# Moving broadcasts, bias blocks and the last loads of an attention stage by a step on one DMA queue

## The chip, the cores and the metric

One kernel runs on one core of a Trainium2 chip. The metric is the device time of one execution in microseconds (us); of several executions the median is taken. The engines are TensorE (PE; its weight loads are PEld), VectorE (DVE), ScalarE (ACT), GpSimd (POOL) and SyncE (SP). SP computes nothing: its queue issues nearly all DMAs of this kernel, in program order, and an issue that must wait holds everything behind it.

## The reference

Two layers in sequence, all in float32.

- Attention with a learned position bias: 4 batches, 8 heads, 576 positions, 64 values a head. The scores are `q k^T / 8` plus a bias that depends on the head and on the two positions: `x = log1p(|i - j|) / log1p(max(i, 1))`, `h = relu(x w1 + b1)` with 32 hidden units, `bias = h w2`. Then a softmax over each row, with `exp(...) / (sum + 1e-9)`, and the product with v.
- A rational expert layer on the 2304 x 512 result x: `h = x w_in` (to 2048), `g = P(h) / (Q(h) + 1e-6)` with a cubic P and a `Q = 1 + |b0| |h| + |b1| h^2`, and `g w_out` (back to 512).

## The kernel before, in words

**Bias stage.** For 36 groups of 16 rows the kernel computes the bias of all heads (`relu` L594 on VectorE and ScalarE, matmuls L640, scaling L646 on ScalarE) and stores it to five tables in DRAM, `tab[0]` to `tab[4]` (L652). The groups are taken in the order 0 to 15, 32 to 35, 16 to 31 (L617), so `tab[4]`, which holds the last 64 rows, is done early. The tile `e` that a store reads has five buffers. `load_bias(p, c)` (L250) reads block c of head pair p from the tables back into an SBUF tile, skewed: three DMAs for c = 0 to 3, six for c = 4. The dictionary `done` (L618) says after which group's store a block of the first pair is read.

**Attention stage.** Heads are taken in pairs; a pair and a batch make a unit u, 16 in all, in the order of pairs. A unit has four blocks of 128 rows; the last 64 rows of two units share a step. So two units take nine steps, a group g, and `step_a(i)` (L498) writes out the work of all 72 steps, NS = 72, as a pipeline: scores of step i (`e_qk` L320, PE L333), bias and row minimum (`e_ttr` L338, DVE L343), exponential with row sums (`e_exp` L352, ACT L359), transposes of step i - 2 (`e_tp` L394) and the product with v of step i - 3 (`e_pv` L430). VectorE copies the products into `xs` (L452; three buffers). The order of the calls is the order on each engine's queue; nothing is reordered.

What each step issues on SP:

- `loads(i)` (L477): q and k of a coming unit (L264, L265; two buffers each), v, a block of the next pair's bias (at steps 2, 5, 8, 10 and 13 of each pair's 18), and at step NS - 7 `load_x(0, 0)` (L277, L283), which reads the first tokens of the attention result back for the expert layer.
- When a unit's last block is through, `e_recip` (L367) inverts its sums, PE transposes them, VectorE copies them to `rt` (L425), and SP writes them to DRAM, `rs` (L428, at the end of the step).
- `load_rb(u)` (L372) reads `rs` back, broadcast to 64 partitions: four DMAs (L378, L382). The first waits until the write of `rs` has landed. In program order it comes one step after that write.
- `e_norm(u)` (L387) multiplies `xs` by the broadcast, on POOL (for u = NX = 12 on VectorE), and SP stores the result, `xd` (L392). It comes five steps after the `load_rb`.
- `run_jobs` (L468) advances a background queue of weight conversion by one VectorE operation a step: loads `wx` and `wy` (L129, L130), operations on VectorE, ScalarE (`wh`, L146) and POOL (L167), and stores of the parts (L171, L107, L108, and L227 for reads of parts stored before).

In the steps i = NS - 5 to NS - 2, `split_x` (L287) splits the first tokens into two parts: a cast on ScalarE (L294, `xh`) ahead of the step's exponentials, and a subtraction on VectorE (L295, `xl`) a step later. At step NS - 1 come `load_x(1, 1)` and the first matmuls of the expert layer, `mm1(0, 0)` (L300, PE L309).

**Expert layer.** It follows from L683 on: 48 sections of h matmuls (L309), rational function on ScalarE, POOL and VectorE, and output matmuls (L770).

Of the kernel before, what the change touches and what calls it, by code (L numbers as in the profile page):

```python
# [33 lines left out]
def tile_attn_moe(  # L34
# [32 lines left out]
    def tab_rows(c, h):  # L67
        n, w, o = P if c < 4 else 64, H * TW - 1, h * TW + S - 1 - P * c
        flat = tab[c].rearrange("r h x -> (r h x)")
        return flat[o:o + n * w].rearrange("(r w) -> r w", w=w)[:, :S]  # L70
# [158 lines left out]
    with tc.manual_schedule():  # L229
# [3 lines left out]
        with ExitStack() as actx:  # L233
# [16 lines left out]
            def load_bias(p, c):  # L250
                if c == 0:
                    bias[p] = bpool.tile([P, 10, S], F32, tag="bias", name=f"bias{p}")
                t = bias[p]
                r0, r1 = tab_rows(c, 2 * p), tab_rows(c, 2 * p + 1)
                for o, x, y, r in ((5 + c, 0, S, r1[:, 0:S]), (c, 64, S, r0[:, 0:512]), (c, 0, 64, r0[:, 512:S])):
                    n = P if c < 4 else 64
                    for z in range(0, P, n):
                        nc.sync.dma_start(out=t[z:z + n, o, x:y], in_=r)

            def load_qk(u, eng=nc.sync):  # L260
                p, b = units[u]
                q = qkp.tile([P, S], F32, tag="q", name=f"q{u}")
                k = qkp.tile([P, S], F32, tag="k", name=f"k{u}")
                eng.dma_start(out=q, in_=qt[b, p])  # L264
                eng.dma_start(out=k, in_=kt[b, p])  # L265
                qk[u] = (q, k)

            def load_v(u, eng=nc.sync):
                p, b = units[u]
                t = vpool.tile([P, 5, P], F32, tag="v", name=f"v{u}")  # L270
                eng.dma_start(out=t, in_=vp[b, p].rearrange("(c k) d -> k c d", k=P))
                vt[u] = t
# [14 lines left out]
            def split_x(n_, k):  # L287
                if k == 0:
                    pool = xps[n_ % 2]
                    xh[n_] = pool.tile([P, KD, TT], F32R, tag="xh", name=f"xh{n_}")  # L290
                    xl[n_] = pool.tile([P, KD, TT], F32R, tag="xl", name=f"xl{n_}")
                hi, lo, x = (v[n_][:, k, :] for v in (xh, xl, xr))
                return (
                    lambda: A.copy(out=hi, in_=x),  # L294
                    lambda: V.tensor_tensor(out=lo, in0=x, in1=hi.bitcast(F32), op=ALU.subtract),  # L295
                )
# [159 lines left out]
            NS = len(steps)  # L456
            later = []
            NU = len(units)
# [18 lines left out]
            def loads(i):  # L477
                g, c = divmod(i, UPG)
                if i == 1:
                    load_qk(1, nc.scalar)  # L480
                    load_v(1, nc.scalar)
                u = 2 * g + 2
                if c == (5 if g else 7) and u < NU:
                    load_qk(u)
                if c == (6 if g else 7) and u < NU:
                    load_v(u)
                if g and c == 0:
                    load_qk(u - 1)
                if g and c == 2:
                    load_v(u - 1)  # L490
                p, r = divmod(i, 2 * UPG)
                r = {2: 0, 5: 1, 8: 2, 10: 3, 13: 4}.get(r)
                if r is not None and p + 1 < NP:
                    load_bias(p + 1, r)
                if i == NS - 7:
                    load_x(0, 0)

            def step_a(i):  # L498
                def ok(d):
                    return 0 <= i - d < NS  # L500

                if i < NS:
                    loads(i)
                first = []
                if NS - 5 <= i < NS - 1:
                    first = split_x(0, i - NS + 5)
                if first:
                    first[0]()
                    later.append(first[1])
                while len(later) > (1 if i < NS - 1 else 0):  # L510
                    later.pop(0)()
                if ok(0):
                    e_qk(i)
                if ok(1):
                    e_exp(i - 1, 1)
                run_act()
                if i >= TL:
                    mx = ps_mx.tile([P, 2, 512], F32, tag="mx", name=f"mx{i}")
                tails = pv = None
                if ok(TL):  # L520
                    tails = e_tp(i - TL, mx)
                if i == NS + 1:
                    mm1(0, 1)
                if ok(TL + 1):
                    pv = e_pv(i - TL - 1, mx)
                if ok(0):
                    for j in range(2):
                        e_ttr(i, j)
                    e_exp(i, 0)
                if ok(1):  # L530
                    u, c = steps[i - 1]
                    if c == (3 if u % 2 else 4):
                        e_recip(u)
                if i == NS - 1:
                    load_x(1, 1)
                    mm1(0, 0)
                g, c = divmod(i - TL, UPG)
                if g > 0:
                    u = 2 * g - 2
                    if c == 1 and u != NX or i == NS + TL:  # L540
                        e_norm(u)
                    if c == 5 and g * 2 < NU:
                        e_norm(u + 1)
                    if c == 0 and u + 1 < NU - 1:
                        load_rb(u + 1)
                if i == NS - 8:
                    e_norm(NX)
                if g < NU // 2 and c == (5 if g else 7):
                    load_rb(2 * g)
                if i >= 2:  # L550
                    run_jobs(i >= 5 and (c > 0 or g % 2 == 0))
                if tails:
                    tails()
                    if i == NS + TL - 1:
                        load_rb(NU - 1)
                if pv:
                    pv()

            with ExitStack() as bctx:
# [55 lines left out]
                bg = in_order(bg, after)  # L615

                order = [*range(16), *range(32, NG), *range(16, 32)]  # L617
                done = {10: 0, 18: 1, 22: 4, 30: 2}  # L618
                for n in order[:LEAD]:
                    relu(n)  # L620
                for y, n in enumerate(order):
                    if y == 4:
                        load_v(0)
                    if y + LEAD < NG:
                        relu(order[y + LEAD])
                    i0 = NROW * n
                    mid = i0 + NROW - 1
                    pool, nm = (ps_sc, "sc")
                    if y == NG - 1:
                        pool, nm = (ps_mx, "mx")  # L630
                    elif y % 3 == 1:
                        pool, nm = (ps_tp, "tp")
                    pa = pool.tile([P, 2, 512], F32, tag=nm, name=f"pb{n}")
                    cuts = sorted({0, mid, 512, EW})
                    for a, z in zip(cuts, cuts[1:]):
                        o = pa[:, a // 512, a % 512:a % 512 + z - a]
                        for c in range(4):
                            x = rows[n, c]
                            x = x[:, a - mid:z - mid] if a >= mid else x[:, mid - a:mid - z:-1]
                            T.matmul(  # L640
                                o[32 * c:32 * c + 32], w28[:, 32 * c:32 * c + 32], x,
                                start=True, stop=True,
                            )
                    e = rpool.tile([P, EW], F32, tag="e", name=f"e{n}")
                    z = 1 if ENG[n][3] == "A" else 0
                    A.activation(  # L646
                        out=e, in_=pa.rearrange("p a s -> p (a s)")[:, :EW], func=AF.Identity,
                        bias=c8[:, z:z + 1], scale=rts[:, n:n + 1],
                    )
                    g, k = divmod(n, 8)  # L650
                    x0 = S - NROW - i0
                    nc.sync.dma_start(  # L652
                        out=tab[g][NROW * k:NROW * k + NROW, :, x0:x0 + EW].rearrange("r h x -> (r h) x"),
                        in_=e,
                    )
                    if y in done:
                        load_bias(0, done[y])
                    if y == NG - 1:
                        load_bias(0, 3)
                    if y >= NG - EARLY:  # L660
                        step_a(y - NG + EARLY)
                A.activation(out=babs, in_=abs_[:, 4:6], func=AF.Abs)
# [274 lines left out]
```

## Time and profile before

| what | value |
|---|---|
| time, median of 3 executions | 731.99 us (731.96 to 733.12) |
| the profiled execution | 728.89 us, of which its span is 727.1 us |
| PE busy | 683.4 us (94% of the span), 6450 instructions |
| DVE busy | 576.1 us (79%) |
| ACT busy | 486.4 us (67%) |
| POOL busy | 232.4 us (32%) |
| mean granted clock of TensorE | 0.981 |
| DMA | 129.69 MB, mean 178 GB/s |

The span runs from the first to the last instruction; the execution's own time is 1.8 us longer. Busy shares are means over the whole span, which has three stages: the bias stage to about 58 us, the attention steps to about 313 us, then the expert layer. Issues of DMAs don't count as busy, so SP has no row here: its work is read from its timeline and from the waits of its queue.

### The profile page before, as it was taken

What the parts mean: (1) busy time and instruction counts of PE and PEld (TensorE: products, weight loads), DVE (VectorE), ACT (ScalarE), POOL (GpSimd) and SP (SyncE); (2) the same over time, 40 slices, a digit from 0 to 9 for tenths busy, and PEclk for the clock granted to TensorE, in tenths of its full rate; (3) what the DMA queues carried; (4) which work ended last, traced back from release to release, by engine and by line L of the source; (5) the groups of instructions that cost most, each with busy time, mean ns of one, the idle gap of its engine ahead of it and who ended that gap; (6) DMA issues with size and microseconds to landing.
All of it is one profiled execution on the core that took longest, in us unless ns stands there. A gap on an engine that the chain in (4) does not pass through costs nothing.

```text
span 727.1 us, 16614 instructions
## 1 busy us (share of the span) xinstructions
PE 683.4 (94%) x6450; PEld 582.7 (80%) x6450; DVE 576.1 (79%) x1032; ACT 486.4 (67%) x758; POOL 232.4 (32%) x144
## 2 busy tenths in 40 slices
PE   6989998979899698699999999999999999999997
PEld 4757876757677586589899998999999999989996
DVE  7976876847677386549999999999986978778766
ACT  6878886868678486567666576766575565656552
POOL 0000221212122120116444545454444444444442
PEclk9999999999999799999999999999999999999999
DMA  4888877877787888625445444369851303032021
GB/s 165 287 293 295 281 225 246 277 235 237 228 279 237 250 275 277 188 87 171 153 142 166 164 136 136 131 189 281 272 172 44 129 2 131 22 109 72 17 87 44
DMA packets 98159, 129.69 MB, mean 178 GB/s; under 512 B 12177, under 2 KB 60577, under 8 KB 98081
## 3 DMA queue, kind: packets, MB, share of 16 engines
q1 hardware_dynamic: 96704, 126.96, 53.5%
q10 hardware_dynamic: 1376, 1.67, 0.7%
q8 instruction: 51, 0.84, 0.5%
q14 instruction: 28, 0.22, 0.1%
HBM read 89.85 MB, written 35.61 MB: 173 GB/s over the span
## 4 chain that ended last, share of the span: by engine, by line
PE 70%; DMA 11%; DVE 4%; issue 2%; SPq 2%; ACT 1%; POOL 0%; DVEq 0%; ACTq 0%; POOLq 0%
PE o L770 26%; PE h L309 26%; PE mx L442 8%; PE sc L333 7%; DMA k<-in_kt_dram 4%; PE tp L402 3%; DMA wih<-wh 2%; DMA rs<-rt 1%; DMA bias<-tab 1%; DMA xd<-xs 1%; DMA ws<-wh 1%; PE mx L402 1%; DVE s L343 1%; DMA xr<-xd 1%; DVE gh L718 1%
## 5 line engine op out<-in xcount | busy, mean ns | idle before, releaser
L343 DVE CUSTOM_DVE_ANT_0 s<-sc,bias 128x576 f32<-128x576 f32 x144 | 103.3, 754 | 57.2 <-PE sc L333 42.3
L700 POOL TENSOR_TENSOR u<-u,w 128x768 f32<-128x768 f32 x48 | 97.2, 2025 | 155.9 <-ACT u L698 155.8
L333 PE MATMUL sc<-k,q 64*128 64x288 f32 (+1 forms) x640 | 96.0, 435 | 17.7 <-DMA k<-in_kt_dram 17.2
L359 ACT ACTIVATE p<-s,m 128x576 f32<-128x576 f32 x144 | 110.5, 771 | 1.3 <-DVE m L343 1.0
L697 ACT ACTIVATE w<-h 128x768 f32<-128x768 f32 x48 | 39.0, 813 | 101.5 <-PE h L309 101.5
L739 POOL TENSOR_TENSOR gl<-m,r 128x768 fp32r<-128x768 f32 x47 | 87.2, 1856 | 55.1 <-DVE m L732 48.7
L410 ACT COPY pt<-tp 128x1024 f32<-128x1024 f32 x72 | 72.6, 1008 | 43.1 <-PE tp L402 42.8
L442 PE MATMUL mx<-pt,v 128*64 128x128 f32 (+1 forms) x1600 | 99.7, 275 | 0.9 <-DVE xs L452 0.9
L309 PE MATMUL h<-xh,wih 128*128 128x384 f32 x288 | 97.3, 338 | 0.0
L309 PE MATMUL h<-xh,wil 128*128 128x384 f32 x288 | 97.0, 337 | 0.0
L309 PE MATMUL h<-xl,wih 128*128 128x384 f32 x288 | 96.9, 336 | 0.0
L442 PEld LDWEIGHTS mx<-pt,v 128*64 128x64 f32 x1600 | 82.7, 142 | 6.3 <-ACT u L698 1.1
L770 PE MATMUL o<-woh,gh 128*128 128x512 f32 x216 | 85.2, 395 | 0.0
L770 PE MATMUL o<-wol,gh 128*128 128x512 f32 x216 | 85.1, 394 | 0.0
L333 PEld LDWEIGHTS sc<-k,q 64*128 64x128 f32 (+1 forms) x640 | 51.9, 179 | 40.2 <-issue 11.8
L704 ACT ACTIVATE r<-u,qc 128x768 f32<-128x768 f32 x48 | 45.1, 940 | 37.3 <-POOL u L700 37.2
L708 DVE TENSOR_TENSOR t<-t,h 128x768 f32<-128x768 f32 x48 | 45.6, 949 | 29.3 <-ACT t L699 23.8
L725 DVE SCALAR_TENSOR_TENSOR m<-u,qc,gh 128x768 f32<-128x768 f32 x48 | 63.0, 1313 | 5.0
L732 DVE SCALAR_TENSOR_TENSOR m<-t,cst,m 128x768 f32<-128x768 f32 x48 | 65.2, 1358 | 1.7
L718 DVE SCALAR_TENSOR_TENSOR gh<-t,cst,r 128x768 fp32r<-128x768 f32 x48 | 53.2, 1109 | 8.2 <-ACT r L705 5.8
L770 PE MATMUL o<-woh,gl 128*128 128x512 f32 x216 | 56.2, 395 | 0.0
L309 PEld LDWEIGHTS h<-xh,wih 128*128 128x128 f32 x288 | 54.1, 188 | 1.8 <-issue 0.3
(71 smaller groups left out, 1286.7 us busy)
## 6 DMA issues: line engine op xcount, KB each, us to landing
tab<-e SPq DMA_DIRECT2D x36, 295.5 KB
wx<-in_w_in_dram SPq DMA_DIRECT2D x16, 512.0 KB
wy<-in_w_in_dram SPq DMA_DIRECT2D x16, 512.0 KB
wx<-in_w_out_dram SPq DMA_DIRECT2D x16, 512.0 KB
wy<-in_w_out_dram SPq DMA_DIRECT2D x16, 512.0 KB
xr<-xd SPq DMA_DIRECT2D x8, 768.0 KB
ws<-wh SPq DMA_DIRECT2D x20, 256.0 KB
ws<-wl SPq DMA_DIRECT2D x20, 256.0 KB
```

The source lines that it names most:

```text
L309: T.matmul(hps[s][:, j, :TT], w[:, k, sl], x[:, k, :], start=(k == 0 and z == 0), stop=(k == KD - 1 and z == 2),)
L333: T.matmul(sc[i, j][o, a, :SH], q[r, x], k[r, a * SH:(a + 1) * SH], start=True, stop=True,)
L343: V.tensor_tensor_reduce(out=t.rearrange("p (a s) -> p a s", a=2), in0=sc.pop((i, j))[:, :, :SH], in1=bias[p][:, 5 * j + c, :].rearrange(" ...
L359: A.activation(out=prob[i][:, z * S:z * S + S], in_=t, func=AF.Exp, bias=m, scale=-1.0, accum_out=sums[u % 4][:, k:k + 1],)
L410: A.copy(out=t[:, 0:8].rearrange("p x (r s) -> p r x s", r=2), in_=ps)
L442: T.matmul(ps[y, o], vt[n][:, kc, y], t[:, 2 * kc + j if kc < 4 else 8, o], start=(kc == 0), stop=(kc == 4),)
L700: G.tensor_tensor(out=u, in0=u, in1=w, op=ALU.mult)
L718: V.scalar_tensor_tensor(out=hi, in0=rt[s, "t"], scalar=abs_[:, 0:1], in1=rt[s, "r0"], op0=ALU.add, op1=ALU.mult,)
L725: V.scalar_tensor_tensor(out=m, in0=rt[s, "u"], scalar=qc, in1=rt[s, "gh"].bitcast(F32), op0=ALU.add, op1=ALU.mult,)
L732: V.scalar_tensor_tensor(out=m, in0=rt[s, "t"], scalar=abs_[:, 0:1], in1=m, op0=ALU.add, op1=ALU.subtract)
L739: eng.tensor_tensor(out=lo, in0=rt[s, "m"], in1=rt[s, "r0"], op=ALU.mult)
L770: T.matmul(po[n, c], l[:, j, c * P:(c + 1) * P], r[fp][:, j, :], start=(first and x is a), stop=(last and x is z),)
```

## The change

No instruction is added or taken away; only places in the order change.

- `load_rb` is called one step later, for odd units (c == 0 to c == 1) and for even ones (c == 5 to c == 6; 7 to 8 in the first group).
- The bias blocks of the next pair are loaded at steps 3, 7, 8, 12 and 16 of a pair's 18, not 2, 5, 8, 10 and 13.
- `load_x(0, 0)`, the four `split_x` of the first tokens and `e_norm(NX)` come one step later each.
- Block 4 of the first pair's bias is read behind block 3, after the last group, not after the 23rd (y = 22).

```diff
--- before.py
+++ after.py
@@ -489,10 +489,10 @@
                 if g and c == 2:
                     load_v(u - 1)
                 p, r = divmod(i, 2 * UPG)
-                r = {2: 0, 5: 1, 8: 2, 10: 3, 13: 4}.get(r)
+                r = {3: 0, 7: 1, 8: 2, 12: 3, 16: 4}.get(r)
                 if r is not None and p + 1 < NP:
                     load_bias(p + 1, r)
-                if i == NS - 7:
+                if i == NS - 6:
                     load_x(0, 0)
 
             def step_a(i):
@@ -502,8 +502,8 @@
                 if i < NS:
                     loads(i)
                 first = []
-                if NS - 5 <= i < NS - 1:
-                    first = split_x(0, i - NS + 5)
+                if NS - 4 <= i < NS:
+                    first = split_x(0, i - NS + 4)
                 if first:
                     first[0]()
                     later.append(first[1])
@@ -541,11 +541,11 @@
                         e_norm(u)
                     if c == 5 and g * 2 < NU:
                         e_norm(u + 1)
-                    if c == 0 and u + 1 < NU - 1:
+                    if c == 1 and u + 1 < NU - 1:
                         load_rb(u + 1)
-                if i == NS - 8:
+                if i == NS - 7:
                     e_norm(NX)
-                if g < NU // 2 and c == (5 if g else 7):
+                if g < NU // 2 and c == (6 if g else 8):
                     load_rb(2 * g)
                 if i >= 2:
                     run_jobs(i >= 5 and (c > 0 or g % 2 == 0))
@@ -615,7 +615,7 @@
                 bg = in_order(bg, after)
 
                 order = [*range(16), *range(32, NG), *range(16, 32)]
-                done = {10: 0, 18: 1, 22: 4, 30: 2}
+                done = {10: 0, 18: 1, 30: 2}
                 for n in order[:LEAD]:
                     relu(n)
                 for y, n in enumerate(order):
@@ -657,6 +657,7 @@
                         load_bias(0, done[y])
                     if y == NG - 1:
                         load_bias(0, 3)
+                        load_bias(0, 4)
                     if y >= NG - EARLY:
                         step_a(y - NG + EARLY)
                 A.activation(out=babs, in_=abs_[:, 4:6], func=AF.Abs)
```

## Rows read from the trace of the kernel before

**Rows 1.** Page, part 4: shares of the chain that ended last, by engine.

```profile
PE 70%; DMA 11%; DVE 4%; issue 2%; SPq 2%; ACT 1%; POOL 0%; DVEq 0%; ACTq 0%; POOLq 0%
```

**Rows 2.** Timeline of PE: start us, us, instructions, [idle before <-releaser].

```profile
64.25 1.24 PE L333 MATMUL sc<-k,q 64*128 64x288 f32 x8
...
108.22 1.24 PE L333 MATMUL sc<-k,q 64*128 64x288 f32 x8 [1.01 <-DMA k<-in_kt_dram]
...
124.04 1.19 PE L333 MATMUL sc<-k,q 64*64 64x288 f32 x14 [2.22 <-DMA k<-in_kt_dram]
...
276.70 1.24 PE L333 MATMUL sc<-k,q 64*128 64x288 f32 x8
...
313.44 0.44 PE L309 MATMUL h<-xh,wih 128*128 128x384 f32 x1
```

**Rows 3.** Waits, 108 to 277 us: who waited for whom: us, times, longest.

```profile
PE sc L333 <- DMA k<-in_kt_dram: 15.6, 7, 6.3
...
PEld sc L333 <- DMA q<-in_qt_dram: 8.2, 3, 4.5
...
PE mx L402 <- DVE xs L452: 4.3, 4, 2.6
...
ACT wh L146 <- DMA wih<-wh: 6.8, 4, 3.4
...
POOL xs L391 <- DMA rb<-rs: 17.6, 4, 6.9
```

**Rows 4.** Waits of SP's own queue, 108 to 277 us.

```profile
SPq L378 <- DMA rs<-rt: 40.4, 11, 4.9
```

**Rows 5.** Timeline of SP: one broadcast and what stands around it; one late broadcast.

```profile
106.92 2.82 SPq L428 DMA_DIRECT2D rs<-rt  x1
109.84 0.37 SPq L392 DMA_DIRECT2D xd<-xs  x1
...
114.14 0.45 SPq L378 DMA_DIRECT2D rb<-rs  x1
...
118.14 0.42 SPq L265 DMA_DIRECT2D k<-in_kt_dram  x1
...
277.56 0.60 SPq L382 DMA_DIRECT2D rb<-rs  x1
```

**Rows 6.** SP's issues by line: count, ns min/median/max, first and last start.

```profile
L258 SPq DMA_DIRECT2D bias<-tab x72: 319/584/1692, 23.0 to 234.9; - x72
...
L129 SPq DMA_DIRECT2D wx<-in_w_in_dram x16: 379/426/1000, 64.8 to 460.6; - x16
```

**Rows 7.** Windows 58:108, 58:313: busy by engine, PEclk, DMA share, GB/s.

```profile
58.00:108.00 50.00, 48.97 (x778) 39.14 (x778) 38.89 (x122) 44.27 (x90) 7.06 (x6) 1.00 0.82 266
58.00:313.00 255.00, 225.46 (x3448) 181.18 (x3450) 174.37 (x538) 190.63 (x377) 44.09 (x33) 0.95 0.78 250
```

**Rows 8.** Timelines of SP, ACT, PE, DVE: block 4 of the first pair, and after.

```profile
38.43 4.61 SPq L258 DMA_DIRECT2D bias<-tab  x6
...
62.02 2.69 SPq L258 DMA_DIRECT2D bias<-tab  x6
...
46.95 1.61 ACT L646 ACTIVATE e<-pb,c,cst 128x591 f32<-128x591 f32 x2 [3.18 <-DMA tab<-e]
...
47.85 5.93 PE L640 MATMUL pb<-ring,w 128*32 128x447 f32 x96 [2.83 <-ACT e L646]
...
49.84 1.27 DVE L602 TENSOR_SCALAR ring<-lts,nts 128x496 f32<-128x496 f32 x3 [1.30 <-PE pb L640]
...
70.37 0.44 DVE L141 TENSOR_SCALAR wk<-wx 128x512 uint32<-128x512 uint32 x1 [0.35 <-DMA wx<-in_w_in_dram]
```

**Rows 9.** Timelines of SP and ACT at the end of attention.

```profile
285.99 0.33 SPq L392 DMA_DIRECT2D xd<-xs  x1
...
292.72 0.57 SPq L283 DMA_DIRECT2D xr<-xd  x1
...
297.96 0.51 ACT L294 CAST xh<-xr 128x384 fp32r<-128x384 f32 x1 [7.54 <-DMA xr<-xd]
```

## The prediction

> **What bounds the kernel now.** I began with the chain of work that ended last: TensorE carries 70% of it and DMAs 11% [rows 1], so beside the matmuls it is transfers that set the end. The windows of the page show TensorE solid from about 360 us on, so the transfers must be on the chain in the attention stage. I read TensorE's timeline there and noted when each of the 72 attention steps starts its scores. From step 4 to step 18 it takes 43.97 us with one wait of 1.01, so 42.96/14 = 3.07 us a step: the pace TensorE can keep. Steps 18 to 64 take 168.48 us where 46 x 3.07 = 141.2 would do: 27.2 us lost. From step 64 to the first matmul of the expert layer it takes 36.74 us where 8 x 3.07 = 24.6 would do: 12.2 us lost [rows 2].
>
> The waits say who is late in that stretch: TensorE waits for k (15.6 us), for q (8.2) and for VectorE's xs copy (4.3); ScalarE waits for the store of an earlier wh before it may write that tile again (6.8 in four waits) [rows 3]. The late parties are SP's DMAs. SP's own waits name the reason: of 169 us it spends 40.4 in 11 waits at L378, for the write of the inverted sums to land before it may read them back as a broadcast [rows 4]. One such place: the rs write is issued until 109.74, one xd store follows, then nothing until the broadcast at 114.14; the k that step 22 needs stands behind it, goes out at 118.14, and TensorE stands still for it until 124.04 [rows 2, 5]. In program order that k belongs to step 18, which began at 108.22: SP runs 10 us behind the step it serves.
>
> **SP's budget** decides. From 108.2 to 277.6 I add up SP's DMA issues: 178 of them take 105 us (the first and the last of them: [rows 5]). With the 40.4 of broadcast waits that is 145.4 us for steps whose matmuls need 141.2. SP can't catch up, whatever it is late by stays, and each further wait of its own (the remaining 24 us) is passed on.
>
> **The change, part by part.**
>
> *Broadcasts a step later.* load_rb issues four DMAs on SP and nothing else. They move behind the jobs of the old step and behind the loads and the xd store of the next; no instruction is added. The rs write needs the same time to land, but SP now issues other DMAs meanwhile. A bias DMA takes 0.584 us at the median, a wx or wy 0.43 [rows 6], an xd 0.37 [rows 5]. For the 11 waits I count what now stands between rs and rb that did not before: six bias DMAs (3.5 us) for rs2, rs6, rs10 (block 4) and for rs4, rs8 (blocks 1 and 2); three bias DMAs and xd (2.1) for rs5, rs9; wx, wy and xd (1.2) for rs3 and rs7; about 1 us of stores or loads for rs11 and rs12, as there is no bias left to load by then. At 3.7 us a wait (40.4/11) that leaves 0.2 us for each of the first five, 1.6 for the next two, 2.5 and 2.7 for the last pairs: 14.6, and with the uneven waits some 16 of the 40.4 us. So 24 us of SP's time are free.
>
> SP then needs 105 + 16 = 121 us for 141 us of steps. It gains nearly 5 us in each group of nine steps, and q and k, issued four steps (12.3 us) before their scores, land in time: k5 took from 118.14 to 124.04, 6 us with its queueing [rows 2, 5]. The stores of wh and xd, late by the same lag, come early too. Bounds for this stretch: all 27.2 us at best; at worst a third of it, 9, if the transfers' own time keeps the rest (first rival). I take 21: SP enters the stretch 8 to 10 us late, so the first waits for k stay in part, and in the last pair, where nothing fills the waits, some come back. The 1.01 us wait ahead of step 18 [rows 2] I count as gone; bounds from 1 slower to 1 faster.
>
> The rs write is out at 109.74 and its reader at 114.14, 4.4 us [rows 5]. The Trainium skill, "DMA: Bandwidth & Descriptors", in its anatomy of one DMA (measured on GpSimd's path), puts the fixed cost at about 2 us, most of it the receipt of the write; the trace here has twice that, with whatever was queued ahead. At 2 us no wait would be left and the stretch would come to its best bound, 6 us under my sum.
>
> *Bias blocks moved* from 2, 5, 8, 10, 13 to 3, 7, 8, 12, 16 of each 18 steps. The same 18 DMAs, all SP's. Taking six of them from in front of the q and k of step 14 and putting them into a wait costs nothing. Block 4 is now loaded six steps (18.4 us) before its use, against a lag of 10, an issue of 3.5 and a landing of 4.4 like that of rs: just covered even if SP never catches up; uncovered, VectorE would wait the shortfall, three times.
>
> *First pair's last block behind the fourth.* Now its six DMAs hold SP from 38.43 for 4.61 us among the table stores; behind them ScalarE waits 3.18 us for a table store to free its buffer, TensorE 2.83 for ScalarE, VectorE 1.30 for TensorE [rows 8]. The gain lies between the 1.30 that reached VectorE and TensorE's 2.83: I take 2.0. At its new place the block's six DMAs (instead of three of the next pair's block 0) stand ahead of the first wx: three DMAs more at 0.45 (2.69/6), 1.35 us. VectorE already waits 0.35 for that wx at 70.37 [rows 8], so I give back 1.4. The block itself is due at step 6, about 71 us; it would be out by 66.1 (62.02 + 9 x 0.45) and landed by 70.5. Sum 0.6 faster; bounds 2.8 faster (no wx wait) and 1.5 slower.
>
> *The end of attention, a step later.* e_norm(12) is one VectorE multiply and an xd store, now issued behind rs13 and v15; load_x is one SP DMA; each of the four splits is a ScalarE cast and a VectorE subtraction. Now xd goes out at 285.99, the read of it at 292.72 and the first cast at 297.96, after ScalarE waited 7.54 us [rows 9]. All three move by one step together, so that chain of 12 us (6.7 for the write to land, 5.2 for the read) stays. With SP on time xd can go out some 4 us into step 65 (an estimate: one step and the multiply), the read lands 16 us into it, and the split of step 68 begins 9.2 us into it: ScalarE still waits 6 to 7 us. That gains 1. Of the 12.2 us lost here 4.7 are more than this wait; I put them down to the lag, as in the stretch before, and count 4. Together 5; bounds 8 faster (half the wait gone as well) and 1 slower (the last split, now in step 71, delays the first matmul). rb14 moves behind two reads of x: hidden, as its multiply comes three steps later; uncovered, it would cost the 2 us of four issues.
>
> Sum: 21 + 1 + 0.6 + 5 = 27.6 us less. The profiled execution took 728.89 us, so 701.3; it lies 3.1 below the median of the runs, 731.99. Taken from the median: **704.4 us**.
>
> **Rivals.**
>
> *The DMA engines bind* (0.20). From 58 to 313 us they are busy 0.78 of 255, 199 us of work; the 70 steps at full pace leave 215, a share of 0.93. In the one long stretch nearly without stalls the share is 0.82 [rows 7]. If that is all these packets allow, 199/0.82 = 243 us instead of 255: a gain of 12, 720 us. Against it: SP's empty waits hold the share down now. The Trainium skill's same page ("Issuing engines are not separate DMA queues") speaks for this rival: time saved on a sequencer is usually small beside the DMA itself; SP's 105 us of issuing in 169 speak against it.
>
> *Slower: the broadcast reaches POOL late* (0.05). POOL multiplies five steps after the broadcast's place, after the change four (12.3 us); it already waits 17.6 us for rb [rows 3]. If SP stays 10 us late, four issues (0.45 to 0.60 each [rows 5]) and a landing of 4.4 make 16.5, and xs is stored 3 us later than now; VectorE's copy then waits for its tile, and TensorE for the copy. If four of the units pass on 3 us each: 12 slower, 744 us. It decides from a lag of about 6 us on. Against it: rb waits for the rs write before and after, so even a late SP issues it hardly later than now.
>
> *No change* (0.09): the waits only move, to the wx loads and wh stores that SP would then reach too early, and q and k stand behind those as they stand behind rb now: 731 us. For it: the 24 us of other waits.
>
> The forecast has 0.66.
>
> **The numbers.** The best bounds together give 731.99 - 27.2 - 1 - 2.8 - 8 = 693; the top must take in the engines' case, 720, with its spread: 694 to 723, the no-change and slower cases left outside. A difference under 0.2% (1.5 us) can't be told from none. Faster: 0.66 + 0.20 + 0.04 of the no-change case; same 0.05; slower 0.05.
>
> **What would show it.** L378's waits in that stretch fall from 40.4 to about 16 us; TensorE's waits for k and q from 24 to under 6; steps 18 to 64 take about 148 us; the 3.18 us wait for a table store is gone; ScalarE's wait before its first xh cast is still 5 to 7 us. I would be wrong if the waits at L378 fell and k still landed late (the engines bind), or if POOL's wait for rb grew and TensorE's waits for xs with it.

## The result and the profile after

The change takes the median from 732.12 to 705.22 us (four executions each, the changed kernel's from 701.93 to 707.14): a ratio of 0.9625, 95% interval 0.9586 to 0.9664, so 26.9 us less, where 27.6 were forecast. The profiled execution after took 701.93 us with a span of 700.1, against 728.89 and 727.1; each lies some 3 us below the median of its kernel.

TensorE's timeline, with the starts that answer to [rows 2]: steps 2, 18, 22 (the part that waits) and 64, and the first matmul of the expert layer.

```profile
54.43 1.67 PE L333 MATMUL sc<-k,q 64*128 64x288 f32 x7 [0.46 <-DVE m L343]
...
104.30 1.24 PE L333 MATMUL sc<-k,q 64*128 64x288 f32 x8
...
120.66 1.71 PE L333 MATMUL sc<-k,q 64*64 64x288 f32 x11 [3.72 <-DMA k<-in_kt_dram]
...
256.00 1.24 PE L333 MATMUL sc<-k,q 64*128 64x288 f32 x8
...
286.39 0.44 PE L309 MATMUL h<-xh,wih 128*128 128x384 f32 x1
```

With step 2 of the kernel before at 58.21 (same view), the span falls apart like this:

| stretch | before, us | after, us | difference | forecast |
|---|---|---|---|---|
| start to step 2 | 58.2 | 54.4 | -3.8 | -2.0 |
| steps 2 to 18 | 50.0 | 49.9 | -0.1 | +0.4 |
| steps 18 to 64 | 168.5 | 151.7 | -16.8 | -21 |
| step 64 to the expert layer | 36.7 | 30.4 | -6.4 | -5 |
| expert layer | 413.7 | 413.7 | 0 | 0 |

Most of the time came from the stretch that was named. That the sum is only 0.7 us off is luck: the stretch brought 4.2 us less than forecast, and the other three rows together 3.7 more. The waits of 104 to 256 us, in the order of [rows 3], and then SP's own, which answers to [rows 4]:

```profile
POOL xs L391 <- DMA rb<-rs: 20.0, 6, 5.4
...
PE sc L333 <- DMA k<-in_kt_dram: 5.4, 2, 3.7
...
ACT wh L146 <- DMA woh<-wh: 3.6, 1, 3.6
...
ACT wh L146 <- DMA ws<-wh: 2.7, 1, 2.7
...
PE mx L402 <- DVE xs L452: 2.2, 3, 1.0
PEld sc L333 <- DMA q<-in_qt_dram: 2.1, 1, 2.1
```

```profile
SPq L378 <- DMA rs<-rt: 6.4, 4, 3.0
SPq L428 <- DVE xs L452: 5.5, 5, 2.2
SPq L130 <- DVE wk L155: 4.6, 3, 2.1
SPq L129 <- DVE xs L452: 4.4, 4, 2.4
```

SP waits 6.4 us for the written sums instead of 40.4, TensorE 7.5 for k and q instead of 23.8 (under 6 was forecast), 2.2 for xs instead of 4.3. SP's other waits grew: all rows of its view add up to 62.5 us before and 53.6 after, so those not at L378 went from 22.1 to 47.2. SP now waits for results of VectorE, as the rows show, and for earlier DMAs to land. POOL's wait for the broadcast grew a little, from 17.6 to 20.0, and TensorE doesn't feel it. The windows tell what else changed, the share of the 16 DMA engines (last column but one) and the granted clock before it: the first two rows are this stretch before and after, the third the end of the bias stage after.

```profile
108.00:277.00 169.00, 148.95 (x2278) 120.03 (x2280) 114.69 (x355) 124.60 (x244) 32.78 (x25) 0.95 0.79 252
```

```profile
104.00:256.00 152.00, 144.15 (x2285) 116.04 (x2281) 116.32 (x359) 125.05 (x247) 33.72 (x25) 0.98 0.90 287
```

```profile
45.00:54.00 9.00, 8.98 (x136) 5.09 (x130) 7.18 (x19) 6.85 (x11) 2.50 (x1) 1.00 0.92 308
```

The engines' share rose from 0.79 to 0.90. TensorE's own busy time (the first figure behind the comma) also fell, by 4.8 us for nearly the same number of instructions, as the granted clock rose from 0.95 to 0.98: 12 us of the stretch's gain are waits that are gone, and some 5 are matmuls that run faster. At the end of the bias stage the row of the kernel before was:

```profile
45.00:54.00 9.00, 6.17 (x99) 2.93 (x100) 5.69 (x15) 6.16 (x9) 0.11 (x1) 0.81 0.89 313
```

A granted clock of 0.81 is a mean of the two levels, 1.2 and 2.4 GHz: TensorE had just stood still for 2.83 us [rows 8], and part of what followed ran at the lower one: taken us by us from 48 to 52, the granted clock was 0.56, 0.50, 0.50 and 0.74. After the change the stall is gone and the clock stays at 1.00.

### The profile page after: what moved, and what is told of

The parts are those of the page before. It is cut to its first block, busy times and chain, and to the rows that moved or that the text cites. A ratio compares the mean times of both kernels' runs of the same rounds, so it can differ in the third digit from the quotient of the medians.

```text
span 700.1 us, 16622 instructions
## 1 busy us (share of the span) xinstructions
PE 676.2 (97%) x6450; PEld 578.4 (83%) x6450; DVE 576.3 (82%) x1032; ACT 485.9 (69%) x758; POOL 235.4 (34%) x144
## 4 chain that ended last, share of the span: by engine, by line
PE 83%; DMA 6%; DVE 5%; issue 2%; ACT 1%; SPq 1%; POOL 0%; DVEq 0%; ACTq 0%; POOLq 0%
PE o L771 27%; PE h L309 27%; PE mx L442 10%; PE sc L333 9%; PE pb L640 5%; PE tp L402 4%; DMA k<-in_kt_dram 1%; DMA tab<-e 1%; PE mx L402 1%; DMA wy<-in_w_in_dram 1%; DVE ring L602 1%; DMA xd<-xs 1%; DMA xr<-xd 1%; SPq L258 1%; ACT p L359 1%
## 5 line engine op out<-in xcount | busy, mean ns | idle before, releaser
L333 PE MATMUL sc<-k,q 64*128 64x288 f32 (+1 forms) x640 | 94.0, 433 | 8.5 <-DMA k<-in_kt_dram 7.9
L442 PE MATMUL mx<-pt,v 128*64 128x128 f32 (+1 forms) x1600 | 96.9, 270 | 0.9 <-DVE xs L452 0.9
L442 PEld LDWEIGHTS mx<-pt,v 128*64 128x64 f32 x1600 | 80.3, 139 | 6.1 <-ACT u L699 1.1
L333 PEld LDWEIGHTS sc<-k,q 64*128 64x128 f32 (+1 forms) x640 | 50.4, 177 | 30.2 <-issue 9.1
L709 DVE TENSOR_TENSOR t<-t,h 128x768 f32<-128x768 f32 x48 | 45.6, 949 | 29.2 <-ACT t L700 23.8
```

The costliest lines, as they stand in the source:

```text
L333: T.matmul(sc[i, j][o, a, :SH], q[r, x], k[r, a * SH:(a + 1) * SH], start=True, stop=True,)
L442: T.matmul(ps[y, o], vt[n][:, kc, y], t[:, 2 * kc + j if kc < 4 else 8, o], start=(kc == 0), stop=(kc == 4),)
```

## The experiments

Each part of the change was tried alone, the broadcasts were taken out of the whole, and the two rivals that could bind were provoked. Ratios are to the kernel before, timed with it on the same chip. In one table, with the stretches taken from the starts of VectorE's reductions (which lie 1.3 to 1.6 us behind TensorE's scores):

```
kernel                 median   ratio (95% interval)      2-18   18-64   64-expert   L378's wait, 18-64
before                 732      1                          49.8   168.4   35.5        40.4
changed                705.22   0.9625 (0.9586-0.9664)     49.7   151.6   29.1         6.4
broadcasts alone       714.30   0.9747 (0.9697-0.9797)     49.3   158.5   31.0        21.1
bias blocks alone      727.76   0.9932 (0.9893-0.9970)     50.0   164.7   35.4        34.0
block 4 alone          733.86   1.0017 (0.9986-1.0049)     56.4   170.3   35.8        42.4
end alone              731.65   0.9994 (0.9962-1.0026)     51.7   170.9   35.7        42.3
all but broadcasts     728.31   0.9922 (0.9887-0.9957)     -      -       -           -
broadcasts from POOL   726.59   0.9911 (0.9874-0.9947)     50.2   164.3   28.8         -
two steps later        702.06   0.9581 (0.9544-0.9619)     51.7   149.4   29.6         0.7
copies from SP         713.45   0.9728 (0.9680-0.9776)     52.8   155.7   32.6         5.5
```

**Which part does the work?** Four kernels, each with one part of the change.

```diff
-                    if c == 0 and u + 1 < NU - 1:
+                    if c == 1 and u + 1 < NU - 1:
...
-                if g < NU // 2 and c == (5 if g else 7):
+                if g < NU // 2 and c == (6 if g else 8):
```

> The kernel before with the broadcasts alone a step later, bias blocks where they were. SP-queue theory: between the write of the sums and its reader some 11 us of other issues come in (in all, over the 11 waits of the stretch from step 18 to step 64), so L378 waits about 30 us there, not 40.4; SP needs 135 us for 141 us of steps and can catch up slowly: about 10 us less in that stretch, 722 us. If the DMA engines bind, under 4 us less, 728 or more. If the late broadcast reaches POOL and nothing fills the wait, slower than before, 735.

Measured: 714.30 us, 17.7 less, nearly twice what was expected and two thirds of the whole. SP's waits and TensorE's, 108 to 267 us:

```profile
SPq L378 <- DMA rs<-rt: 21.1, 9, 4.7
```

```profile
PE sc L333 <- DMA k<-in_kt_dram: 10.7, 3, 5.3
...
PEld sc L333 <- DMA q<-in_qt_dram: 3.4, 1, 3.4
```

Half of SP's waiting at L378 is gone (19 of 40 us, where 11 were counted), and with it 9.9 us of the stretch, as much as was expected for it. What was not expected is the end: it is 4.5 us shorter too, although only the broadcasts of units 13 and 14 move there, and those had waited 0.5 us. So the end was late mostly because SP was.

```diff
-                r = {2: 0, 5: 1, 8: 2, 10: 3, 13: 4}.get(r)
+                r = {3: 0, 7: 1, 8: 2, 12: 3, 16: 4}.get(r)
```

> The kernel before with the bias blocks of the next pair alone moved to steps 3, 7, 8, 12, 16. SP-queue theory: block 4 and block 1 come between rs and its reader (about 14 us less waiting), block 0 leaves its place there (3.5 more): L378 waits about 30 us, again some 10 us less in all, 722 us; so the blocks do half of the work, not the broadcasts alone. Rival (the broadcast's own step is what counts, the blocks only make room): no change, 731.

Measured: 727.76 us, 0.68% less, 4.2 us where 10 were expected. L378 still waits 34.0 us in 8 waits (40.4 in 11): the blocks alone end three waits and lengthen others. The blocks don't do half of the work; alone they bring a quarter of what the broadcasts bring alone.

```diff
-                done = {10: 0, 18: 1, 22: 4, 30: 2}
+                done = {10: 0, 18: 1, 30: 2}
...
                         load_bias(0, 3)
+                        load_bias(0, 4)
```

> The kernel before with only the first pair's block 4 read behind block 3. Step 2 begins 3.8 us earlier (54.4 us, as in the changed kernel) because no table store is late; about 1 us goes back at steps 5 to 7, where VectorE waits for the first wx. Theory: from then on the stretch is as before, 729 us. Rival: in the changed kernel the 3.8 us also came from elsewhere, and here step 2 begins at 56 us or later.

Measured: 733.86 us, no gain. The start is as expected, step 2 is reached 3.5 us earlier. But steps 2 to 18 take 6.6 us more, not 1, and 4.2 of them show at one wait. SP's timeline and VectorE's:

```profile
58.90 7.35 SPq L258 DMA_DIRECT2D bias<-tab  x12
66.30 0.43 SPq L129 DMA_DIRECT2D wx<-in_w_in_dram  x1
```

```profile
71.11 0.43 DVE L141 TENSOR_SCALAR wk<-wx 128x512 uint32<-128x512 uint32 x1 [4.59 <-DMA wx<-in_w_in_dram]
```

Twelve bias DMAs stand ahead of the first wx: blocks 3 and 4, and block 0 of the next pair, still at step 2. VectorE waits 4.59 us for that wx. In the changed kernel block 0 has moved behind it (step 3), nine stand ahead, and the wait is 1.47:

```profile
67.71 0.43 DVE L141 TENSOR_SCALAR wk<-wx 128x512 uint32<-128x512 uint32 x1 [1.47 <-DMA wx<-in_w_in_dram]
```

So this part is worth nothing alone; in the changed kernel, where the blocks make room, its 3.8 us at the start are kept. No run took this part alone out of the whole change, so what it is worth there is not shown.

```diff
-                if i == NS - 7:
+                if i == NS - 6:
                     load_x(0, 0)
...
-                if NS - 5 <= i < NS - 1:
-                    first = split_x(0, i - NS + 5)
+                if NS - 4 <= i < NS:
+                    first = split_x(0, i - NS + 4)
...
-                if i == NS - 8:
+                if i == NS - 7:
                     e_norm(NX)
```

> The kernel before with only load_x, the four splits and e_norm(12) a step later. Theory: SP's lag was what made the end late (steps 64 to the first matmul of the expert layer took 36.7 us before, 30.4 in the changed kernel), so with the lag still there this part alone gives 1 us, 731. Rival: the later split takes ScalarE's wait away by itself, 5 us or more, 727.

Measured: 731.65 us, the same as before. The stretch from step 64 on is no shorter (35.7 us against 35.5), though ScalarE's wait ahead of the first cast fell from 7.54 to 3.74 us; TensorE then waits for k and q there instead (11.7 us). This part gives nothing by itself.

**Without the broadcasts.** The whole change but for the two lines of the first experiment.

> The changed kernel with the broadcasts put back one step earlier; everything else of the change stays. SP-queue theory: L378's waits between steps 18 and 64 come back to some 34 us, that stretch takes 163 to 166 us, and the end is late again: 721 to 725 us, where the changed kernel takes 705. Rival (the order at the start and at the end does most of it): 712 or less.

Measured: 728.31 us, 0.78% less than before and 23 more than the changed kernel, 3 us above the expected range. With the broadcasts at their old place, the rest of the change is worth no more than the blocks alone. Its profiled execution took 735.36 us, so only its time is used here, none of its rows.

**Is it SP's waiting, or the waiting as such?** The kernel before with nothing moved, but the four broadcast DMAs issued from POOL.

```diff
-                    nc.sync.dma_start(
+                    nc.gpsimd.dma_start(
                         out=o[:, 0:512].rearrange("d (c s) -> d c s", c=4),
...
-                    nc.sync.dma_start(
+                    nc.gpsimd.dma_start(
                         out=o[:, 512:S],
```

> The kernel before, with nothing moved, but the four broadcast DMAs issued from POOL's queue, so that POOL and not SP waits for the sums to land. SP-queue theory: SP loses 40 us of waits and 44 issues (27 us) between steps 18 and 64; that stretch falls from 168 to 150 us or less, 710 us or below in all, although the same bytes move. If the DMA engines bind: over 155 us for the stretch and at least 718. If POOL, which now waits and issues as well, is late with its multiplications, TensorE's waits for VectorE's xs copy grow.

Measured: 726.59 us, a ratio of 0.9911: the 710 of the theory failed. The time lies where the rival for the engines had it, but for another reason. The waits of 108 to 274 us, SP's first:

```profile
SPq L392 <- POOL xs L391: 28.6, 6, 7.1
```

```profile
POOL rb L378 <- DMA rs<-rt: 82.9, 11, 12.2
...
PE mx L402 <- DVE xs L452: 16.7, 7, 5.5
ACT wh L146 <- DVE wk L141: 15.0, 6, 7.7
DVE wk L141 <- POOL wl L167: 11.1, 2, 8.8
DVE wk L141 <- POOL wol L167: 8.9, 3, 5.6
...
PE sc L333 <- DMA k<-in_kt_dram: 3.1, 2, 2.2
```

With SP rid of the broadcasts and of their wait, k is late for 3.1 us where it was 15.6, no wait for q is left on the list, and the end takes 28.8 us instead of 35.5: that half of the theory holds. SP's queue still waits, though: 28.6 us for POOL's products, which its xd stores need, and 94.5 us in all, where it was 62.5. But the wait for the sums didn't vanish; POOL has it now, and POOL's queue holds the subtractions of the weight conversion (L167). VectorE waits 20 us for those, and TensorE 16.7 for VectorE. Here the wait that was moved to another queue is paid by what stands behind it there. The change before us fills the wait with work instead.

**Later still.** The changed kernel with the broadcasts another step later (`c == 2`, and `c == 7` for even units but the first).

> The changed kernel with the broadcasts another step later (the first group's even unit stays). SP-queue theory: only 6.4 us of waits at L378 are left between steps 18 and 64 and SP has time to spare, so taking them away gives 0 to 2 us: 703 to 706. Rival (a later broadcast reaches POOL): POOL multiplies three steps after the broadcast, its waits for rb grow from 20 to over 35 us in that stretch, xs tiles come free late, and TensorE's waits for xs grow from 2 to over 8: 711 or more.

Measured: 702.06 us (700.77 to 704.19), ratio 0.9581, a little below the range of the SP-queue theory. POOL's row is as the rival has it, and TensorE's is not (106 to 256 us):

```profile
POOL xs L391 <- DMA rb<-rs: 52.4, 10, 13.8
...
PE mx L402 <- DVE xs L452: 2.5, 3, 1.0
```

POOL waits 52.4 us for the broadcasts, and TensorE 2.5 us for xs, about as before this edit (2.2). The rival's mechanism is there, but it does not reach TensorE even at twice the delay.

**Do the DMA engines bind now?** The changed kernel with 12 copies of 320 KB that nobody needs.

```diff
                 eng.dma_start(out=t, in_=vp[b, p].rearrange("(c k) d -> k c d", k=P))
+                if u >= 4:
+                    z = dpool.tile([5 * P, P], F32, tag=f"z{u}", name=f"z{u}")
+                    eng.dma_start(out=z, in_=vp[b, p])
```

> The changed kernel with one DMA more for each of the units 4 to 15: behind the load of v, 320 KB are copied from DRAM to a scratch in DRAM that nobody reads (3.9 MB read and written). If the DMA engines bind now: the copies are some 12 to 15 us of their time at the rates of this stage, and 8 us or more of it show, 713 or above. If SP's queue alone bound: 12 issues of some 0.45 us in its spare time, under 2 us, 707 or less. Between these: the engines' backlog has become a part of what is left.

Measured: 713.45 us, 8.2 more than the changed kernel. SP doesn't run short: it waits only 5.5 us at the broadcasts, and it still has some 40 us between steps 18 and 64 in which it issues nothing (the stretch less the rows of its timeline). TensorE waits for k and q again:

```profile
PE sc L336 <- DMA k<-in_kt_dram: 7.7, 3, 3.2
...
PEld sc L336 <- DMA q<-in_qt_dram: 3.7, 1, 3.7
```

(The inserted lines shift the numbers by three.) So 12 more copies cost time now, at a share of 0.91 of the engines. Of the two profiled executions, steps 2 to 18 differ by 3.1 us, nearly all of it before the first copy goes out at 101.2 us, so that part is not theirs; 4.1 us fall in steps 18 to 64, with ten copies, and 3.5 behind them. Nor are the engines shown to be full at 0.90: with the broadcasts two steps later they run at 0.94 over the stretch, and the kernel is not slower. To ask the same of the kernel before, and without SP's issues, the copies went to ScalarE's queue in both (`nc.scalar.dma_start`).

> The kernel before with the same 12 copies of 320 KB to a scratch nobody reads, but issued from ScalarE's queue, so that SP issues nothing more. If SP's waits bound the kernel before and the 16 engines stood idle in them (share 0.79), the copies run in those gaps: 0 to 3 us more, 732 to 735. If the engines bound already: 8 us or more, 740.

> The changed kernel with the 12 copies issued from ScalarE's queue. The copies on SP's queue cost 8 us (713.45 against 705.22). If it is the engines' time (share 0.90 in the changed kernel): again 6 to 10 us, 711 to 715, and more than they cost the kernel before. If it was SP's 12 issues: 707 or less.

Measured: 742.22 us (1.0141, interval 1.0113 to 1.0168) and 719.02 us (0.9819, 0.9790 to 0.9848), 10.3 and 13.8 more. By the text on record that says "the engines" for both, though 719.02 lies above the 711 to 715 of that case; and the pair doesn't decide it, because the issue itself disturbs ScalarE. Its timeline in the kernel before with copies:

```profile
166.34 0.19 ACT L362 ACTIVATION_READ_ACCUMULATOR p<-s,m 128x1 f32 x1
176.67 0.52 ACTq L274 DMA_DIRECT2D z<-in_vp_dram  x1
177.23 0.77 ACT L362 ACTIVATE p<-s,m 128x576 f32<-128x576 f32 x1 [10.69 <-DMA bias<-tab]
```

ScalarE stands still for 10 us before it issues the copy, and the next exponential waits behind it. What the issue waits for isn't named by the profile in a way that I could confirm. So for the kernel before, whether more bytes alone would have cost it time stays open.

**A version that beats both?** Two more built on the later broadcast: unit 12's broadcast left where the change put it, and then also block 4's six DMAs spread over the bias stage.

```diff
-                if g < NU // 2 and c == (6 if g else 8):
+                if 0 <= g < NU // 2 and c == (8 if g == 0 else 6 if 2 * g == NX else 7):
                     load_rb(2 * g)
...
+                    if y in (20, 22, 24, 26, 28, 32):
+                        load_bias(0, 4, (20, 22, 24, 26, 28, 32).index(y))
...
-                        load_bias(0, 4)
```

> The changed kernel with the broadcasts another step later, but unit 12's, which VectorE reads at the end, left where the change put it. Another step later took 702.06, with a wait of 4.2 us at that one; without it the end is 2 to 4 us shorter: 698 to 700. If the engines' backlog sets the end, no gain: 702.

> The same, with the six DMAs of the first pair's block 4 spread one by one between the table stores (after groups 20, 22, 24, 26, 28 and 32 of the order), not behind block 3. Theory: no store is held up for long, so step 2 still begins at about 56 us, and the first wx is no longer late: 1 to 2 us less than without the spread, 697 to 699. Rival: the table stores fill the engines there, each block DMA delays one, step 2 begins 1 us or more later, and nothing is gained.

Measured: 702.33 us (0.9592, interval 0.9567 to 0.9618) and 701.75 us (0.9571, 0.9536 to 0.9607). The first gains nothing over 702.06: its end is as long as without the edit, 29.5 us against 29.6. The second makes step 2 start 2.4 us later (58.3 against 55.9 us at VectorE) as its rival had it, and gains that back in steps 18 to 64; no net gain that can be told. All three later versions lie 3 us below the changed kernel's median, with intervals that overlap its own, so "a little faster than the change" is likely and not shown.

## Why the prediction was right, and where its terms were off

**SP's budget** was the right ground for the stretch, though two terms of it were mis-sized. The 40.4 us of waits at L378 were what SP could not afford: filling them took k and q off TensorE's waits, and the broadcasts alone, which add and remove no instruction, gave two thirds of the gain. The broadcast experiments bracket it: with the wait put back 23 of the 26.9 us are gone (728), with the broadcasts off SP's queue k comes in time (3.1 us of waiting), though POOL pays. One reading of the page was off without consequence: its slices show TensorE at nine tenths from 309 us on, not from about 360.

**What remains of the waits** was set at 16 us and is 6.4. The size that failed is that of the filler, above all where three bias DMAs or wx, wy and xd were to fill the wait: rs3, rs5, rs7 and rs9 were given 8.2 us of waiting and have 2.1. For rs3 and rs9 the issues between the write and its broadcast took 4.6 and 5.0 us, where their medians give some 3.4 and 2.5. SP's timeline after, with rs2, shows the same:

```profile
100.59 0.72 SPq L428 DMA_DIRECT2D rs<-rt  x1
101.35 6.01 SPq L258 DMA_DIRECT2D bias<-tab  x6
...
109.14 0.44 SPq L378 DMA_DIRECT2D rb<-rs  x1
...
113.66 0.42 SPq L265 DMA_DIRECT2D k<-in_kt_dram  x1
```

The six bias DMAs take 6.01 us where 3.5 were counted: the issues themselves are 3.7, and two of them wait before they go out, 1.2 us for a wy and 0.9 for a v to land; the xd behind them waits 1.3 for a wih. Nothing is left to wait for at L378, but most of the 3.8 us that were waited there has only changed its place in SP's queue.

**Steps 18 to 64** were given 21 us and brought 16.8, the largest miss. The step that failed: I let SP's free time become TensorE's, short of a residue of 6.2 us (27.2 less 21). The residue is 10.5 us (151.7 against 46 x 3.07). SP did not get all that time: of the 34 us that left L378, 25 came back in its other waits, though how far those held up k and q is not shown. And the lag at the entry cost more than was set: the k above belongs to step 18, which began at 104.30; it goes out 9.4 us into it (9.9 before), step 22 starts its part with it at 120.66, 7 us later, and loses 3.72 us where it had lost 2.22. Beside it ScalarE waits 3.6 us, until 121.26, for a store of wh to land. TensorE stands still meanwhile, and the granted clock falls to its lower level; the engines are full there (1.09; a packet's whole time counts where it starts):

```profile
119.00:125.60 6.60, 4.94 (x48) 3.58 (x50) 2.05 (x5) 2.22 (x3) 0.00 (x0) 0.50 1.09 377
```

By VectorE's starts, steps 21 and 22 take 12.3 us where 6.1 would do, over half of the residue. The first rival's reading, that the engines cannot exceed 0.82, is refuted by their 0.90. That the bytes are now a part of the bound, as it held in kind, is likely from the 8 us of the 12 copies, and not shown. The Trainium skill ("DMA: Bandwidth & Descriptors", "Issuing engines are not separate DMA queues") says that the time saved on a sequencer is usually small beside the DMA itself. It means the time to start a DMA, and the run that gave the four issues to another engine fits that: 0.9% less time. The 17.7 us of the broadcasts alone are another thing, a wait ahead of an issue.

**The bias stage**: 2.0 was taken between 1.30 and 2.83, and 3.8 came, above the upper bound. The term left out is TensorE's clock: the window with the 2.83 us stall and what follows it had a granted 0.81 and has 1.00 now. That the clock makes up the whole 0.95 us above the stall is argued from these rows; no run tried it by itself. The **give-back** at the first wx was 1.47 us of waiting against 0.35, so 1.1 for the 1.4 set.

**The end**: the chain is as long as set, xd at 262.82, its read at 269.63, the cast at 274.87, 12 us. ScalarE's wait is 2.51 us and not 6 to 7, as step 68 itself is late by a wait for k15 at step 67 (2.06 us). The gain of 6.4, set at 5, is mostly SP's recovered lag and not the moved lines: these alone gave nothing, and the broadcasts alone shortened the end by 4.5 us.

**Rivals**: the late broadcast did not reach TensorE, at one step (POOL's waits 17.6 to 20.0) or at two (52.4). "The waits only move" is what happened when they were handed to POOL, and in part on SP's own queue (22.1 to 47.2 us away from L378), but there k and q came earlier all the same.

## What to carry to other kernels

Add up an in-order DMA queue's issue time and its waits per period, and compare the sum with the period of the engine it serves: here 145.4 us stood against 141.2, SP could not catch up, and later loads inherited a lag of some 10 us, however early they stood in the program. A wait for a round trip through DRAM can be filled with other issues that are due anyway, placed between the write and the read (40.4 us fell to 6.4); look also at what the queue waits for after that. Handing the wait to another queue handed it to what stood behind it there. Test the parts together as well as alone: a part that is worth nothing alone, like block 4's new place here, may pay once another makes room for it.

## What the runs showed that I had not expected

- The broadcasts alone were worth 17.7 us and the bias blocks alone 4.2, where the count of DMAs between write and read had given both the same 10.
- POOL can wait 52.4 us of 149 for its broadcasts without TensorE noticing: its multiplication then comes three steps behind the broadcast.
- A copy issued from ScalarE's queue held ScalarE for up to 10 us before it went out; what it waited for is open.
- Taking away a stall of 2.83 us brought 3.8 us: the window around it had a mean granted clock of 0.81, and has 1.00 without it. In steps 18 to 64 as well, some 5 of the 17 us are faster matmuls.
